# Weights' loads issued from ScalarE, new estimates for a planner, and short chunks of keys filled up, in an attention and MLP kernel

## The chip, the cores and the metric

One core of one Trainium2 chip. The metric is device time in microseconds of one execution, median over runs: 1034.23 us for the kernel before (1033.37 to 1034.86, three runs).

## The reference, cut to what matters

Inputs: local queries, keys and values (8 batches, 8 heads, 512 positions, 64 features), global ones (32 positions), and two weight matrices, 512 x 2048 and 2048 x 512, which arrive as 64-bit floats.

```python
k_all = concat([k_g, k_l]); v_all = concat([v_g, v_l])
out_g = softmax(scale * q_g @ k_all.T) @ v_all              # global queries see all keys
s_ll  = where(|i - j| <= 32, scale * q_l @ k_l.T, -1e9)     # local ones a band
s_l   = concat([scale * q_l @ k_g.T, s_ll])                 # and the 32 global keys
out_l = softmax(s_l) @ v_all
x = concat([out_g, out_l]) as (8 * 544 tokens, 8 heads * 64)
h = x @ w_in                                               # 512 -> 2048
g = h * tanh(softplus(h))                                  # mish
return g @ w_out                                           # 2048 -> 512
```

## The kernel before

**Tiling.** Heads are taken in pairs (`hp`, 4 for each batch `b`), called a head below. A unit is 128 local queries `t` of one head, 128 units in all. `scores` (lines 599 and 606) multiplies queries with a window of 192 or 224 key columns; `row_max` (VectorE), `expo` (ScalarE), `p_hi` and `p_lo` make two 16-bit parts `ph` of the probabilities; `p_turn` transposes them into `pt` by DMA; `pv` (line 657) multiplies `pt` with two chunks of values: `va` (rows by `CHK`: 96, 128, 128, 128 for the four tiles) and `vc` (96, 96, 96, 64), each with three products for high and low parts, in two halves of the head pair. That makes 12 small matmuls of 64 moving columns for a unit. `v_move` fills `va` and `vc` by DMA from `vf` and `vgf`. The global queries run once for each head: `g_scores`, `g_max`, `g_exp`, `g_norm`, `g_turn`, and `g_pv` (line 744), whose first chunk has 32 rows (partitions 96 to 127 of `va` and of `gpt`) and whose other four have 128.

**MLP.** Tokens go in 17 blocks of 256. For each block 8 steps: `m1_mm` (line 787), `mish` on ScalarE (line 830), `g_hi` and `g_lo`, `m2_mm` (line 855).

**Weights.** 32 halves of 512 KB each, 0 to 15 of the first matrix and 16 to 31 of the second. `w_load` brings one in by `load`, a DMA issued on the sync engine's queue (SP, line 294); `w_bits` and `w_sum` make 32-bit floats of it on VectorE, ScalarE and GpSimd; `w_stat` and `w_norm` work out a scale, with a reduction over partitions on GpSimd (line 414); `w_split` writes two 16-bit parts. Their raw bits lie in buffers that other tiles use later (`PLACE`). Batches' values have a scale too, by `b_max` and `b_scale` (reduction at line 490), used by `b_split` (line 510).

**Order.** `Plan` simulates the engines when the program is built: each task has an engine, a duration in ns, what it reads and writes, and a priority (its number, or, with `pl.slot`, a place counted in units of 37 tasks). `order` (line 133) takes the task that can start soonest, at equal time the one of lowest priority; the instructions of each engine are then put out in that order and each engine runs them in order, waiting where it must. DMAs are a fifth engine there, "DMA", issued on SP: one occupies it for `max(ns, DMA_MIN)` and is done `DMA_IN + ns + DMA_OUT` after its start (lines 191 to 193). A task on VectorE beside GpSimd is lengthened (line 190). The constants at lines 1013 to 1027 say where the weights' steps and the loads of later batches are placed.

Of the kernel before, what the change touches and what calls it, by code (L numbers as in the profile page):

```python
# [12 lines left out]
F16 = mybir.dt.float16  # L13
# [30 lines left out]
CHK = [(96, 96), (128, 96), (128, 96), (128, 64)]  # L44
# [6 lines left out]
class Plan:  # L51
# [5 lines left out]
    DMA_IN, DMA_OUT, DMA_MIN = 1650, 900, 650  # L57
# [75 lines left out]
    def order(self):  # L133
# [10 lines left out]
        columns = {}  # L144

# [17 lines left out]
        def first(e):  # L163

            best = None
            for pri, n, ns, t in queue[e]:
                t = max(t, free[e]) + (self.TABLE if e == ACT and self.tasks[n][7] not in (None, self.table) else 0)
# [12 lines left out]
        for _ in range(N):  # L180
            t, pri, e, n, ns = min(c for c in map(first, free) if c)
            start[n], on[n] = t, e
            if e == ACT:
                self.table = self.tasks[n][7] or self.table
# [4 lines left out]
            if e == DVE and free[POOL] > t:  # L189
                ns += 0.5 * min(ns, free[POOL] - t)  # L190
            if e == DMA:
                free[e] = t + max(ns, self.DMA_MIN)
                done[n] = t + self.DMA_IN + ns + self.DMA_OUT
            else:
                free[e] = done[n] = t + ns
# [19 lines left out]
def attn_mish_kernel(ctx: ExitStack, tc: tile.TileContext, qt, kt, qt0, kt0, vm, vg, qg, w1, w2, consts_in, out, w64):  # L215
    nc = tc.nc
# [19 lines left out]
    def rings(pool, *table):  # L236
        for tag, bufs, shape, dt in table:
# [11 lines left out]
          ("vf", 2, [128, 4, 2, 128], F16), ("va", 2, [128, 4, 2, 128], F16), ("vc", 2, [96, 4, 2, 128], F16),  # L249
# [14 lines left out]

    def kept(tag, bufs, shape):
# [5 lines left out]
    kept("ph", 2, [128, 2, 2, 256])  # L271
    kept("gph", 1, [64, 2, 640])
# [85 lines left out]
    def w_load(k):  # L358
        j, hf = HV[k]

        def go():
            n = 2 if w64 else 1
            dst = raw(k) if w64 else wf(k).bitcast(I32)
            if j < 8:
                load(dst.rearrange("p (c f) -> p c f", c=2),
                     w1[hf * 256:(hf + 1) * 256, j * 256 * n:(j + 1) * 256 * n].rearrange("(c p) f -> p c f", p=128))
            else:
                r0 = (j - 8) * 256 + hf * 128
                load(dst, w2[r0:r0 + 128, :])
        if w64:  # L370
            p = PLACE[k]
            pl.add(DMA, dma(512), go, w=[rawkey(k)] if p in range(18) else (), new=() if p in range(18) else [(p, ("wraw", k))])
        else:
            pl.add(DMA, dma(256), go, w=[wkey(j, hf)])
# [3 lines left out]
    def w_bits(k):  # L378
# [3 lines left out]
        pl.add(DVE, 335, lambda: V.tensor_scalar(f(), words(k)[:, :, 1], 3, 0x3FFFFFFF, ALU.logical_shift_left, ALU.bitwise_and),  # L382
# [4 lines left out]
    def w_sum(k):  # L387
# [3 lines left out]
        pl.add(DVE, 602, lambda: V.scalar_tensor_tensor(f(), words(k)[:, :, 1], -0x40000000, f(), ALU.bitwise_and, ALU.bitwise_or),  # L391
               r=[rawkey(k)], w=[key])
        pl.add(POOL, pool(512), lambda: G.tensor_tensor(f(), f(), X["wr", k], ALU.add), r=[("wr", k)], w=[key])  # L393
# [13 lines left out]
    def w_norm(w):  # L407
# [6 lines left out]
        pl.add(POOL, 600, lambda: G.partition_all_reduce(X[p], X[m], 128, RED.add), r=[m], new=[("p2", p)])  # L414
# [15 lines left out]
    def w_split(j):  # L430
# [9 lines left out]
        else:  # L440
            pl.add([(ACT, act(1024)), (DVE, dve2(1024))], 0, lambda e: scaled(e, f, f, c), r=[["sw", w]], w=[k])
            pl.add([(ACT, act(1024)), (DVE, dve2(1024))], 0, lambda e: copy(e, wh(j, 0), f), r=[k], w=[wslot(j)])
            pl.add(POOL, pool(1024) * 0.9, lambda: G.tensor_tensor(wh(j, 1), f, wh(j, 0), ALU.subtract), r=[k, hi], w=[lo])
# [701 lines left out]
```

## Time and profile before

| | us |
|---|---|
| median of three runs | 1034.23 |
| the profiled execution | 1032.9 |
| its span, first to last instruction | 1031.1 |
| TensorE busy (matmul) | 944.5, 92% |
| ScalarE busy | 681.1, 66% |
| VectorE busy | 665.0, 64% |
| GpSimd busy | 81.8, 8% |
| mean granted TensorE clock | 0.994 |

Line 855 and line 787 (the MLP) hold about 1050 us of matmul records that overlap one another, line 657 123 us, line 744 26 us. The shares are averages: the first fifth of the span looks different from the rest, so the profile is read by stretches of 20 us. All DMAs of the program run on one queue. In the rows PE is TensorE's matmul, PEld its weight load, DVE VectorE, ACT ScalarE, POOL GpSimd, SPq the issue of DMAs on the sync engine. In brackets stands the idle time of the engine ahead of a group and what ended it.

### The profile page before, as it was taken

How to read it: one execution, taken by the hardware profiler on the slowest of the kernel's cores; microseconds unless marked ns; L12 is line 12 of the kernel's file. 1: busy time of each engine (PE TensorE's matmuls, PEld its weight loads, DVE VectorE, ACT ScalarE, POOL GpSimd, SP SyncE). 2: the span in 40 equal slices, each digit the busy share in tenths (PEclk: the TensorE clock that was granted, in tenths of full speed). 3: DMA queues.
4: the chain of work that ended last, by engine and by line, in shares of the span. 5: the costliest groups of instructions: out<-in, count | busy, mean ns of one | idle time of the engine just before them, and what ended most of it. 6: DMA issues, size and time to landing. Idle time of an engine off the chain costs nothing.

```text
span 1031.1 us, 20578 instructions
## 1 busy us (share of the span) xinstructions
PE 944.5 (92%) x7906; PEld 670.3 (65%) x7906; DVE 665.0 (64%) x1704; ACT 681.1 (66%) x1321; POOL 81.8 (8%) x60
## 2 busy tenths in 40 slices
PE   3456797899999999999999999999999999999996
PEld 2234475566776777777767777777777777666663
DVE  6877896887667766776676666767676655422221
ACT  3465566666887788778878788787878788311110
POOL 2725222410000000000000000000000000000000
PEclk9999998999999999999999999999999999999998
DMA  9847983696758764766566665665576444100000
GB/s 333 220 115 171 281 233 78 121 187 155 165 105 176 144 143 105 182 141 141 116 163 148 131 131 129 159 128 133 119 162 125 116 75 79 38 11 21 1 21 21
DMA packets 231802, 134.65 MB, mean 131 GB/s; under 512 B 197528, under 2 KB 209048, under 8 KB 230680
## 3 DMA queue, kind: packets, MB, share of 16 engines
q1 hardware_dynamic: 231704, 133.34, 56.6%
q8 instruction: 62, 1.02, 0.4%
q14 instruction: 36, 0.29, 0.1%
HBM read 63.55 MB, written 8.91 MB: 70 GB/s over the span
## 4 chain that ended last, share of the span: by engine, by line
PE 71%; DVE 11%; DMA 7%; issue 2%; ACT 2%; SPq 1%; POOL 0%; ACTq 0%; DVEq 0%
PE o L855 29%; PE h L787 29%; PE U L657 4%; PE s L606 4%; DMA vraw<-in_vm 3%; PE g L695 2%; PE gu L744 2%; DMA gpt<-gph 2%; DVE vmx L479 1%; DMA pt<-ph 1%; DVE ph L640 1%; DVE P L612 1%; DVE ks L300 1%; DVE kl L544 1%; DMA wraw<-in_w 1%
## 5 line engine op out<-in xcount | busy, mean ns | idle before, releaser
L855 PE MATMUL o<-W,G 128*128 128x512 f16 x1632 | 389.9, 379 | 0.0
L787 PE MATMUL h<-xh,W 128*128 128x256 f16 x2048 | 379.3, 275 | 5.2 <-ACT e L830 5.1
L787 PEld LDWEIGHTS <-W 128*128 128x128 f16 x3264 | 310.9, 98 | 69.8 <-issue 5.5
L787 PE MATMUL h<-xl,W 128*128 128x256 f16 x1024 | 281.0, 274 | 0.0
L855 PEld LDWEIGHTS <-G 128*128 128x128 f16 x1632 | 156.8, 98 | 144.3 <-issue 0.3
L830 ACT ACTIVATE e<-h,c 128x512 f32<-128x512 f32 (+1 forms) x137 | 92.6, 683 | 117.0 <-PE h L787 115.9
L621 ACT ACTIVATE P<-P,nm 128x192 f32<-128x192 f32 (+1 forms) x256 | 117.8, 460 | 40.3 <-DVE nm L612 39.0
L612 DVE CUSTOM_DVE_ANT_0 P<-s,consts 128x192 f32<-128x192 f32 (+1 forms) x256 | 90.1, 367 | 79.3 <-PE s L606 70.2
L307 DVE TENSOR_SCALAR G<-e,c 128x512 f16<-128x512 f32 x129 | 63.2, 490 | 115.3 <-ACT e L830 115.1
L640 DVE SCALAR_TENSOR_TENSOR ph<-P,ph 128x384 f16<-128x384 f32 (+1 forms) x128 | 79.1, 619 | 82.0 <-ACT ph L305 81.3
L843 DVE SCALAR_TENSOR_TENSOR G<-e,c,G 128x512 f16<-128x512 f32 (+1 forms) x137 | 102.0, 744 | 3.4
L830 ACT ACT_TABLE_LOAD x79 | 101.4, 1283 | 1.4
L621 ACT ACT_TABLE_LOAD x74 | 94.9, 1283 | 1.4
L657 PEld LDWEIGHTS <-pt 96*128 96x128 f16 (+2 forms) x1536 | 64.1, 101 | 34.2 <-DMA pt<-ph 21.6
L305 ACT ACTIVATE ph<-P 128x384 f16<-128x384 f32 (+1 forms) x128 | 69.7, 547 | 16.3 <-DMA pt<-ph 13.2
L657 PE MATMUL U<-va,pt 128*128 128x64 f16 (+1 forms) x768 | 62.0, 200 | 14.8 <-DMA pt<-ph 12.5
L606 PE MATMUL s<-ks,qs 128*128 128x192 f32 (+1 forms) x216 | 71.4, 353 | 1.4 <-DVE qs L536 0.8
L657 PE MATMUL U<-vc,pt 96*128 96x64 f16 (+1 forms) x768 | 61.3, 198 | 0.0
L393 POOL TENSOR_TENSOR W<-W,wr 128x512 int32<-128x512 int32 x32 | 50.2, 1579 | 77.3 <-DVE W L391 42.4
L716 ACT ACTIVATE gP<-g,gmx 64x288 f32<-64x288 f32 x64 | 30.4, 476 | 37.8 <-DVE gmx L711 37.6
L606 PE MATMUL s<-kl,qs 128*128 128x192 f32 (+1 forms) x216 | 54.2, 274 | 0.0
L403 PE MATMUL ws<-W 128*128 128x128 bf16 x128 | 17.7, 285 | 37.0 <-POOL W L393 37.0
(102 smaller groups left out, 1016.6 us busy)
## 6 DMA issues: line engine op xcount, KB each, us to landing
kraw<-in_kt SPq DMA_DIRECT2D x27, 640.0 KB, 4.7
qraw<-in_qt SPq DMA_DIRECT2D x27, 512.0 KB, 4.1
W<-in_w SPq DMA_DIRECT2D x19, 512.0 KB, 6.1
out<-ob SPq DMA_DIRECT2D x34, 256.0 KB, 2.6
vraw<-in_vm SPq DMA_DIRECT2D x8, 1024.0 KB, 6.1
wraw<-in_w SPq DMA_DIRECT2D x13, 512.0 KB, 6.2
vc<-vf SPq DMA_DIRECT2D x32, 128.0 KB, 2.3
va<-vf SPq DMA_DIRECT2D x32, 96.0 KB, 2.3
```

Source lines behind the costliest of these rows:

```text
L305: A.activation(out=dst, in_=src, func=AF.Copy, scale=c)
L307: V.tensor_scalar(dst, src, c, None, ALU.mult)
L393: pl.add(POOL, pool(512), lambda: G.tensor_tensor(f(), f(), X["wr", k], ALU.add), r=[("wr", k)], w=[key])
L606: T.matmul(X[s][:, :w], X[qs][:, h, t * 128:(t + 1) * 128], X[k][:, h, c0:c0 + w], start=(i == 0), stop=(i == 1))
L612: pl.add(DVE, 69 + 1.04 * w, lambda: V.tensor_tensor_reduce(out=X[P][:, h, :w], in0=X[s][:, :w], in1=mask[:, m0:m0 + w], scale=-SCALE, sca ...
L621: pl.add(ACT, 160 + 0.832 * w + 93, lambda: A.activation(out=X[P][:, h, :w], in_=X[P][:, h, :w], func=AF.Exp, bias=X[nm], scale=-1.0, accu ...
L640: pl.add(DVE, dve(n), lambda: V.scalar_tensor_tensor(p_part(X[ph], t, 1), p_src(X[P], t), PSC, p_part(X[ph], t, 0), ALU.mult, ALU.subtract ...
L657: T.matmul(X[u][:, t, h, :], X[pt][:k, p * 4 + h * 2 + c, :], X[vx][:k, t, vl, h * 64:(h + 1) * 64], start=(n == 0), stop=(n == 5))
L787: T.matmul(X[h][:, f * TB:(f + 1) * TB], wh(i, wl)[:, off:off + 128], X[x][:, d, o:o + TB], start=(n == 0), stop=(n == 11))
L830: chain(blk, i, ACT, 571, lambda a, z: A.activation(out=X[e][:, a:z], in_=hv(blk, i)[:, a:z], func=AF.Mish, bias=0.0, scale=X[c][:, 0:1]), ...
L843: chain(blk, i, DVE, 602, lambda a, z: V.scalar_tensor_tensor(gp(1, blk, i)[:, a:z], X[e][:, a:z], X["c", blk][:, 2:3], gp(0, blk, i)[:, a ...
L855: T.matmul(X[o], gp(g, blk, i)[:, f, t * 128:(t + 1) * 128], wh(8 + i, wl)[:, f * 512:(f + 1) * 512], start=(i == 0 and n == 0), stop=(i = ...
```

## The change

Four parts. `w_load` issues its DMA from ScalarE, and the planner holds it for a task of ScalarE of the kind "dma", with an account of its own for the bytes moved. The planner's durations are set anew: DMA constants, transposes 8 ns for each KB instead of 5, the two reductions over partitions 4500 ns instead of 600, several steps of the weights, the lengthening beside GpSimd; and the constants that place the weights' steps and later batches' loads. The last tile's second chunk in `CHK` has 96 rows instead of 64, and `g_pv` multiplies all 128 rows of its first chunk instead of 32. For that, `vc` is a kept tile that is cleared once at the start, so rows that no move fills are zero; the first 96 columns of `gph` were cleared already.

```diff
-CHK = [(96, 96), (128, 96), (128, 96), (128, 64)]
+CHK = [(96, 96), (128, 96), (128, 96), (128, 96)]
-    DMA_IN, DMA_OUT, DMA_MIN = 1650, 900, 650
+    DMA_IN, DMA_OUT, DMA_MIN, DMA_AHEAD = 1300, 600, 620, 4000
...
+            if self.tasks[n][7] == "dma":
+                moved2 = max(moved2, t) + ns * 1.2
+                free[e] = t + self.DMA_MIN
+                done[n] = moved2 + self.DMA_IN + self.DMA_OUT
...
             if e == DVE and free[POOL] > t:
-                ns += 0.5 * min(ns, free[POOL] - t)
+                ns += 0.6 * min(ns, free[POOL] - t)
             if e == DMA:
-                free[e] = t + max(ns, self.DMA_MIN)
-                done[n] = t + self.DMA_IN + ns + self.DMA_OUT
+                moved = max(moved, t) + ns
+                free[e] = max(t + self.DMA_MIN, moved - self.DMA_AHEAD)
+                done[n] = moved + self.DMA_IN + self.DMA_OUT
...
-          ("vf", 2, [128, 4, 2, 128], F16), ("va", 2, [128, 4, 2, 128], F16), ("vc", 2, [96, 4, 2, 128], F16),
+          ("vf", 2, [128, 4, 2, 128], F16), ("va", 2, [128, 4, 2, 128], F16),
...
     kept("ph", 2, [128, 2, 2, 256])
+    kept("vc", 2, [96, 4, 2, 128])
     kept("gph", 1, [64, 2, 640])
...
             if j < 8:
-                load(dst.rearrange("p (c f) -> p c f", c=2),
+                nc.scalar.dma_start(dst.rearrange("p (c f) -> p c f", c=2),
...
             else:
                 r0 = (j - 8) * 256 + hf * 128
-                load(dst, w2[r0:r0 + 128, :])
+                nc.scalar.dma_start(dst, w2[r0:r0 + 128, :])
...
-            pl.add(DMA, dma(512), go, w=[rawkey(k)] if p in range(18) else (), new=() if p in range(18) else [(p, ("wraw", k))])
+            pl.add(ACT, dma(512), go, w=[rawkey(k)] if p in range(18) else (), new=() if p in range(18) else [(p, ("wraw", k))], table="dma")
...
-        pl.add(POOL, 600, lambda: G.partition_all_reduce(X[p], X[m], 128, RED.add), r=[m], new=[("p2", p)])
+        pl.add(POOL, 4500, lambda: G.partition_all_reduce(X[p], X[m], 128, RED.add), r=[m], new=[("p2", p)])
...
-        pl.add(DMA, kib * 5, lambda: nc.sync.dma_start_transpose(dst(), src()), r=r, w=w, new=new)
+        pl.add(DMA, kib * 8, lambda: nc.sync.dma_start_transpose(dst(), src()), r=r, w=w, new=new)
...
-        pl.add(POOL, 600, lambda: G.partition_all_reduce(X[p], X[m][:, 5:6], 128, RED.max), r=[m], new=[("p2", p)])
+        pl.add(POOL, 4500, lambda: G.partition_all_reduce(X[p], X[m][:, 5:6], 128, RED.max), r=[m], new=[("p2", p)])
...
             for c in range(5):
-                r = slice(0, 128) if c else slice(96, 128)
-                vv = X[vf][:, c - 1] if c else X[va][r, 1]
+                vv = X[vf][:, c - 1] if c else X[va][:, 1]
                 for p, vl in ((0, 0), (0, 1), (1, 0)):
-                    T.matmul(X[u][:, :64], vv[:, vl, :], X[pt][r, p * 5 + c, :], start=(n == 0), stop=(n == 14))
+                    T.matmul(X[u][:, :64], vv[:, vl, :], X[pt][:, p * 5 + c, :], start=(n == 0), stop=(n == 14))
...
-    RATE1 = 0.1
-    CONV2 = 8.279
+    RATE1 = 0.133
+    CONV2 = 7.324
...
-    FIRST1 = 10.551
-    STEP1 = 0.114
-    FIRST2 = 14.027
+    FIRST1 = 9.986
+    STEP1 = 0.14
+    FIRST2 = 13.099
     STEP2 = 0.833
-    AHEAD_DMA = 3.119
-    LATE_K = 11.02
-    LATE_L = 158.572
-    LATE_B = 8.569
-    LATE_V = 0.0
+    LOAD1 = -1.233
+    LOADS1 = 0.116
+    AHEAD_DMA = 7.181
+    LATE_K = 122.989
+    LATE_L = 168.71
+    LATE_B = 0.0
+    LATE_V = 294.429
...
         if a == "w":
+            pl.slot = LOAD1 + LOADS1 * n
             w_load(n)
+            pl.slot = None
```

## Rows read from the trace of the kernel before

**Rows 1.** Stretches of 20 us: PE, PEld, DVE, ACT, POOL busy; PEclk; DMA share; GB/s.

```profile
0.00:20.00 20.00, 9.32 (x26) 5.29 (x26) 11.99 (x40) 8.51 (x22) 3.78 (x8) 1.00 0.89 318
20.00:40.00 20.00, 8.75 (x46) 4.93 (x46) 15.95 (x31) 8.60 (x20) 14.08 (x10) 1.00 1.11 328
40.00:60.00 20.00, 6.47 (x40) 3.70 (x38) 13.62 (x29) 6.49 (x18) 8.47 (x7) 1.00 0.28 68
...
120.00:140.00 20.00, 16.59 (x113) 11.58 (x113) 19.19 (x40) 10.79 (x25) 7.68 (x6) 1.00 1.09 291
...
160.00:180.00 20.00, 14.87 (x125) 10.87 (x123) 12.09 (x32) 14.84 (x21) 3.91 (x4) 0.83 0.36 75
...
200.00:220.00 20.00, 17.99 (x144) 11.09 (x143) 14.82 (x43) 15.24 (x35) 4.29 (x2) 1.00 0.90 187
...
500.00:520.00 20.00, 20.00 (x183) 14.56 (x181) 14.27 (x37) 16.61 (x32) 0.00 (x0) 1.00 0.49 105
...
sum 1040.00, PE 944.52 PEld 670.27 DVE 665.01 ACT 681.07 POOL 81.79; mean PE 18.16 PEld 12.89 DVE 12.79 ACT 13.10 POOL 1.57
```

**Rows 2.** Timeline of TensorE, 506 to 515 us: start, duration, line, operation.

```profile
506.78 0.26 PE L657 MATMUL U<-va,pt 128*128 128x64 f16 x3
...
507.14 0.27 PE L787 MATMUL h<-xh,W 128*128 128x256 f16 x1
...
508.45 1.46 PE L855 MATMUL o<-W,G 128*128 128x512 f16 x6
509.75 0.27 PE L787 MATMUL h<-xh,W 128*128 128x256 f16 x1
...
511.06 1.46 PE L855 MATMUL o<-W,G 128*128 128x512 f16 x6
512.45 0.26 PE L744 MATMUL gu<-gpt,va 32*128 32x64 f16 x3
...
513.00 0.35 PE L606 MATMUL s<-ks,qs 128*128 128x224 f32 x1
...
513.52 0.26 PE L657 MATMUL U<-va,pt 128*128 128x64 f16 x3
...
514.29 0.28 PE L787 MATMUL h<-xh,W 128*128 128x256 f16 x1
```

**Rows 3.** Groups by line and shape, whole span: busy us, mean ns | idle.

```profile
L657 PE MATMUL U<-vc,pt 64*128 64x64 f16 x192 | 17.1, 198 | 0.0
...
L744 PE MATMUL gu<-gpt,va 32*128 32x64 f16 x96 | 8.5, 196 | 1.7 <-DMA gpt<-gph 1.7
```

**Rows 4.** Line 744 alone in stretches of 20 us: PE, PEld, PEclk, DMA.

```profile
200.00:220.00 20.00, 0.71 (x15) 0.54 (x15) 1.00 0.90 187
```

**Rows 5.** Timeline of GpSimd at the start.

```profile
0.72 1.84 POOL L268 MEMSET ph<- 128x1024 f16 x2 [0.29 <-POOLq L1134]
```

**Rows 6.** Timeline of all engines around 58 us, at the weights' first reduction.

```profile
58.23 0.15 DVE L415 TENSOR_SCALAR wp<-wp 128x1 f32<-128x1 f32 x1 [4.32 <-POOL wp L414]
...
58.74 1.01 PE L599 MATMUL s<-ks,qs 64*128 64x192 f32 x2 [4.25 <-DVE nm L612]
```

**Rows 7.** Timelines of ScalarE and of TensorE around 165 us.

```profile
164.40 0.40 ACT L510 ACTIVATE vgf<-vgraw,sv 128x128 f16<-128x128 f32 x1 [7.72 <-DVE sv L315]
...
166.65 0.37 PE L787 MATMUL h<-xh,W 128*128 128x256 f16 x1 [5.09 <-ACT e L830]
```

**Rows 8.** Chain that ended last, in order of time, 110 to 240 us.

```profile
166.65 8.18 PE h L787 x48
```

**Rows 9.** Instructions of wraw (min/median/max ns), then timeline of SP's issues and VectorE.

```profile
L294 SPq DMA_DIRECT2D wraw<-in_w x13: 328/577/1452, 4.2 to 137.2; - x13
...
18.16 5.11 SPq L294 DMA_DIRECT2D W<-in_w  x5
30.48 7.84 SPq L465 DMA_TRANSPOSE pt<-ph  x2
...
8.54 0.56 DVE L640 SCALAR_TENSOR_TENSOR ph<-P,ph 128x384 f16<-128x384 f32 x1
```

More of the change, by code (lines that the diff above doesn't have):

```diff
@@ L144, in order @@
         columns = {}
+        moved = moved2 = 0
         def tensor(t, ns, rows):
@@ L166, in first @@
             for pri, n, ns, t in queue[e]:
-                t = max(t, free[e]) + (self.TABLE if e == ACT and self.tasks[n][7] not in (None, self.table) else 0)
+                t = max(t, free[e]) + (self.TABLE if e == ACT and self.tasks[n][7] not in (None, "dma", self.table) else 0)
                 e0 = self.tasks[n][0][0][0]
@@ L182, in order @@
             start[n], on[n] = t, e
+            if self.tasks[n][7] == "dma":
+                moved2 = max(moved2, t) + ns * 1.2
+                free[e] = t + self.DMA_MIN
+                done[n] = moved2 + self.DMA_IN + self.DMA_OUT
+                queue[e] = [c for c in queue[e] if c[1] != n]
+                for u in users[n]:
+                    left[u] -= 1
+                    if not left[u]:
+                        enter(u)
+                continue
             if e == ACT:
@@ L368, in go @@
                 r0 = (j - 8) * 256 + hf * 128
-                load(dst, w2[r0:r0 + 128, :])
+                nc.scalar.dma_start(dst, w2[r0:r0 + 128, :])
         if w64:
             p = PLACE[k]
-            pl.add(DMA, dma(512), go, w=[rawkey(k)] if p in range(18) else (), new=() if p in range(18) else [(p, ("wraw", k))])
+            pl.add(ACT, dma(512), go, w=[rawkey(k)] if p in range(18) else (), new=() if p in range(18) else [(p, ("wraw", k))], table="dma")
         else:
-            pl.add(DMA, dma(256), go, w=[wkey(j, hf)])
+            pl.add(ACT, dma(256), go, w=[wkey(j, hf)], table="dma")
     def w_bits(k):
@@ L381, in w_bits @@
         f, key = lambda: wf(k).bitcast(I32), wkey(*HV[k])
-        pl.add(DVE, 335, lambda: V.tensor_scalar(f(), words(k)[:, :, 1], 3, 0x3FFFFFFF, ALU.logical_shift_left, ALU.bitwise_and),
+        pl.add(DVE, 360, lambda: V.tensor_scalar(f(), words(k)[:, :, 1], 3, 0x3FFFFFFF, ALU.logical_shift_left, ALU.bitwise_and),
                r=[rawkey(k)], w=[key])
@@ L390, in w_sum @@
         f, key = lambda: wf(k).bitcast(I32), wkey(*HV[k])
-        pl.add(DVE, 602, lambda: V.scalar_tensor_tensor(f(), words(k)[:, :, 1], -0x40000000, f(), ALU.bitwise_and, ALU.bitwise_or),
+        pl.add(DVE, 680, lambda: V.scalar_tensor_tensor(f(), words(k)[:, :, 1], -0x40000000, f(), ALU.bitwise_and, ALU.bitwise_or),
                r=[rawkey(k)], w=[key])
-        pl.add(POOL, pool(512), lambda: G.tensor_tensor(f(), f(), X["wr", k], ALU.add), r=[("wr", k)], w=[key])
+        pl.add(POOL, 1400, lambda: G.tensor_tensor(f(), f(), X["wr", k], ALU.add), r=[("wr", k)], w=[key])
     def w_stat(k):
@@ L442, in w_split @@
             pl.add([(ACT, act(1024)), (DVE, dve2(1024))], 0, lambda e: copy(e, wh(j, 0), f), r=[k], w=[wslot(j)])
-            pl.add(POOL, pool(1024) * 0.9, lambda: G.tensor_tensor(wh(j, 1), f, wh(j, 0), ALU.subtract), r=[k, hi], w=[lo])
+            pl.add(POOL, 2230, lambda: G.tensor_tensor(wh(j, 1), f, wh(j, 0), ALU.subtract), r=[k, hi], w=[lo])
     LO, HI = slice(0, 64), slice(64, 128)
```

## The prediction

> **What bounds the kernel now.** I read the stretches of 20 us first, for which engine is full where. From 220 us to the end TensorE is busy for the whole of nearly every stretch: 20.00 of 20.00 in 500 to 520, at a granted clock of 1.00, 2.4 GHz [rows 1]. VectorE (14.27) and ScalarE (16.61) have room there. Before that TensorE is half idle: 9.32, 8.75 and 6.47 us of the first three stretches, 14.87 of 160 to 180 [rows 1]. Over the span it is busy 944.52 us of 1031.1, so it idles 86.6 us, and the eleven stretches up to 220 us, of which the first and the last stand in the rows, hold 72.4 of these. The end can therefore come sooner in two ways only: TensorE gets less work after 220 us, or it waits less before. I look at the first with the timeline of TensorE in the steady part, at the second with the waits and the timeline of the start.
>
> **Filling the short chunks.** The timeline of TensorE shows two prices for the same twelve instructions. Line 657 makes four groups of three small products for each tile of 128 queries. Tiles whose chunks have 128 and 96 rows: first start at 506.78, next work at 507.14, so 0.36 us, 0.030 each. The last tile of a head, with chunks of 128 and 64 rows: 513.52 to 514.29, 0.77 us [rows 2]. Going from 128 to 96 rows costs nothing; going to 64 rows and back costs about 0.1 us each time, and the last tile does so four times. Filling the 64 to 96 makes it a tile like the others: 0.77 - 0.36 = 0.41 us less for each head.
>
> Line 744 starts with three products of 32 rows. It takes from 512.45 to 513.00, 0.55 us for 15 products; at 0.030 each it would be 0.45, so 0.10 of that is the way back to 128 rows. The way there lies ahead of it: six products of line 855 that are followed by a 128-row product take 508.45 to 509.75, 1.30 us, those that are followed by the 32-row ones 511.06 to 512.45, 1.39 us, 0.09 more [rows 2]. Together 0.19 us for each head, and 0.60 with the tile above. There are 192 matmuls with 64 rows and 96 with 32 rows, six and three for each of 32 heads [rows 3]; their count stays, only their rows grow, and I cost the added rows at nothing, since 96- and 128-row products already run at the same 0.030.
>
> Heads in the full part: six stretches up to 220 us hold 15 matmuls of line 744 each, the last of them that of [rows 4], so 6 of the 32 groups lie before and 26 after. 26 x 0.60 = **15.6 us less**, one for one, since no other engine is near full there. What covers this: ScalarE at 16.61 of 20 goes to about 17. For the other 6 heads (3.6 us) TensorE waits anyhow; I take 0 and keep 0 to 3.6. Padding also needs zeroed rows in vc: two more clears on GpSimd. The two clears of ph, of the same length per partition, take 1.84 us at the very start [rows 5], where nothing has landed that GpSimd could work on; hidden. Without that cover it would be 1.8 us once.
>
> The Trainium skill (TensorEngine Tiling (Array Packing), Key Properties) says that a change of tiling mode drains the engine, which the 0.1 us agrees with. The same page (Theoretical Speedup) speaks against filling: 64 and 32 rows may run up to 2 and 4 times faster. By it the change would forfeit 192 x 0.015 + 96 x 0.022 = 5 us, an estimate from that page; no group in the trace shows such a speed-up.
>
> **The planner's estimates.** The planner builds the order of every engine from its own durations, so a wrong one puts an instruction that must wait in front of others on an in-order engine. It gave the reduction over partitions 600 ns. In the trace VectorE idles 4.32 us until the weights' first one is done, and TensorE 4.25 us at the same place [rows 6]. The second is worse: ScalarE waits 7.72 us at line 510 for a scale from the next reduction, and behind it in its queue is the mish whose result TensorE needs; TensorE idles 5.09 us, and the next 48 products of line 787 run partly at the lower level of the clock, 1.2 GHz (0.83 on average in 160 to 180) [rows 1, 7]. They take 8.18 us [rows 8], where the steady rate is 1.31 for 12 (511.06 less 509.75 [rows 2]), 5.2 for 48, so 2.9 lost. Sum of what the right estimate (4500 ns) could remove: 4.25 + 5.09 + 2.9 = 12.2 us. The other way the bound is a plan that helps nowhere, 0. I take half, **6 us less**: when these waits are filled VectorE is next, with 15.95 of 20 in 20 to 40 and 19.19 in 120 to 140 [rows 1], and work moved into a gap still has to be work that TensorE was waiting for. The other estimates (transposes, splits, vector operations beside GpSimd) and the new places of the weights' steps only change this same order; they have no rows of their own, and their spread goes into the range.
>
> **The weights' loads on ScalarE.** 32 instructions leave SP's queue and enter ScalarE's. On SP one takes 0.33 to 1.45 us, 0.58 at the median [rows 9]: 32 x 0.58 = 18.5 us of ScalarE's time, 10.5 to 46 at the ends. The first sixteen are the dear ones: five took 5.11 us [rows 9], because the DMA engines were full: 318 and 328 GB/s in the first two stretches [rows 1]. ScalarE is busy 8.51, 8.60 and 6.49 us of the first three stretches [rows 1], so there is room, but each load stands in order: what is queued behind it on ScalarE is the exponentials of the first tiles and the low words of the weights, for which the probabilities' transposes and GpSimd's sums wait. Loads 16 to 31 also wait until a buffer is read out; on SP transposes were behind them, now the exponentials and the mish are. In return SP is free: in the trace the first two transposes of probabilities are issued at 30.48 and take 7.84 us, although a first low part of ph is written at 8.54 [rows 9]; loads and moves stood before them. Bounds: a gain up to the TensorE idle time of 20 to 60 us, 24.8 us [rows 1]; a loss up to 16 x 1.45 = 23 us. I take **0**: nearest are the rows of these stretches, in which the DMA engines, not an issuing queue, were full until 40 us.
>
> Sum against the profiled execution, 1032.9 us (span 1031.1 and 1.8 around it): 1032.9 - 15.6 - 6 = 1011.3. The median of the runs is 1.3 us above that execution, so **1012.6**, I say 1012.
>
> **Rivals.**
> *The plan books two queues, the chip has one set of engines.* The new planner keeps a separate account for ScalarE's loads, as if they moved beside SP's. In the first two stretches 318 and 328 GB/s [rows 1] were the sum of all. Sixteen loads of 0.52 MB are 8.4 MB, 26 us at 323 GB/s; keys, queries and values of batch 0, about 3.8 MB by their shapes in the code, are 12 us more. Booked side by side they end at 26, on the chip at 38, so work placed by the plan may wait up to 12 us on ScalarE and VectorE. Then the 6 us are gone and up to 12 added: 1034.2 - 15.6 + (0 to 12) = 1019 to 1031, middle 1025. For it: every early step hangs on loads. Against it: in the kernel before the loads took as long, and VectorE was behind them anyway. The Trainium skill states the rule (DMA: Bandwidth & Descriptors, Issuing engines are not separate DMA queues): issuing from another engine saves only the issue time; the trace of before has all its loads on one queue and can't show it.
>
> *The start gets much better.* SP's freedom lets the first tiles' results come tens of us sooner, and with them the first layer. All 12.2 us, the 3.6 and a third of the 24.8: 1034.2 - 15.6 - 12.2 - 3.6 - 8 = 995. Against it: VectorE's fill.
>
> *ScalarE blocks (slower than before).* At its place, the first 25 us, the loads hold ScalarE as long as they held SP at worst, 16 x 1.45 = 23 us, and no exponential gets in between; all of batch 0 shifts by that. With the 15.6 and without the 6: 1034.2 + 23 - 15.6 = 1042. It decides for slower once the shift is over 15.6 us. Against it: ScalarE is idle for more than half of these stretches, and the plan places first tiles' exponentials by their order among the loads.
>
> *The filling doesn't remove the price:* if the 0.1 us came from the weight loads of another tensor and not from the row count, the 15.6 would stay; then 1034.2 - 6 = 1028. Against it: 128 to 96 rows changes the tensor too and costs nothing [rows 2].
>
> **How the numbers follow.** Forecast, 1003 to 1018: 0.60. Two queues booked, 1018 to 1031: 0.21. Start much better, under 1003: 0.12. Filling worth nothing: 0.03, most of it near no change. Slower: 0.04. The range for 8 in 10: 1000 to 1026; it takes in the forecast, half of the much better start and most of the second case. A measurement of this kernel can tell about 0.2% from no change: faster 0.93, same 0.03, slower 0.04.
>
> **What would show it.** In the profile after: line 657's 64-row form and line 744's 32-row form are gone, and the last tile of a head goes by in 0.36 us; TensorE's full part is 15 us shorter. VectorE's and ScalarE's waits for a reduction of 4 to 8 us are gone or cover nothing of TensorE. Idle time of TensorE up to 220 us falls from 72 to about 66. Loads are listed on ScalarE's queue at 0.3 to 1.5 us each, with its first exponential near 7 us still; if that comes after 15 us, the blocking case holds. The prediction is wrong if TensorE's early idle time moves by over 12 us either way, or if ScalarE becomes full after 220 us.

## The result and the profile after

The changed kernel takes 1037.41 us (median; 1034.86 to 1039.48) where the kernel before takes 1034.23. The ratio is 1.0025, with a 95% interval of 1.0013 to 1.0037: a little slower. The forecast was 1012 us. The profiled execution has a span of 1037.7 us, 1039.48 as a run: it is the slowest of the thirteen, 2.1 us above the median, while the profiled one of the kernel before lies 1.3 below its median. So 3.4 us of what the two profiles differ by are spread between runs.

The price of a tile in the steady part went as forecast. The timeline of TensorE (start, us, engine, line, operation, out<-in, shape, count), the last tile of a head, line 657 before and 671 now:

```profile
511.13 0.26 PE L671 MATMUL U<-va,pt 128*128 128x64 f16 x3
511.23 0.25 PE L671 MATMUL U<-vc,pt 96*128 96x64 f16 x3
511.32 0.25 PE L671 MATMUL U<-va,pt 128*128 128x64 f16 x3
511.40 0.25 PE L671 MATMUL U<-vc,pt 96*128 96x64 f16 x3
511.50 0.27 PE L800 MATMUL h<-xh,W 128*128 128x256 f16 x1
```

0.37 us in place of 0.77 [rows 2]. The groups by line and shape hold the 64- and 32-row products of [rows 3] no more:

```profile
L671 PE MATMUL U<-vc,pt 96*128 96x64 f16 x768 | 58.9, 198 | 0.0
...
L757 PE MATMUL gu<-gpt,va 128*128 128x64 f16 x96 | 8.4, 199 | 2.2 <-DMA gpt<-gph 2.1
```

The start went otherwise. Stretches of 20 us, columns as in [rows 1]:

```profile
0.00:20.00 20.00, 4.76 (x16) 2.75 (x16) 10.07 (x24) 2.61 (x3) 6.63 (x11) 1.00 0.93 347
20.00:40.00 20.00, 3.26 (x14) 1.65 (x14) 4.25 (x12) 3.74 (x10) 2.60 (x3) 1.00 1.04 393
...
100.00:120.00 20.00, 10.00 (x94) 6.86 (x91) 19.94 (x32) 13.01 (x25) 10.20 (x5) 0.50 0.89 210
120.00:140.00 20.00, 10.84 (x73) 6.61 (x72) 19.83 (x47) 12.38 (x31) 9.07 (x6) 0.50 0.71 161
160.00:180.00 20.00, 15.59 (x119) 12.80 (x118) 13.42 (x40) 16.92 (x24) 3.23 (x3) 0.83 0.30 82
...
500.00:520.00 20.00, 20.00 (x175) 14.91 (x173) 14.53 (x42) 17.39 (x31) 0.00 (x0) 1.00 0.52 110
```

In the first 40 us TensorE is busy 8.0 us where it was 18.1, VectorE 14.3 where it was 27.9, ScalarE 6.4 where it was 17.1. Then VectorE is full from 100 to 140 us, and TensorE's clock is at its lower level there. Why the start is empty shows on three engines. ScalarE, with its own issues (ACTq):

```profile
0.75 5.64 ACTq L379 DMA_DIRECT2D wraw<-in_w  x4
7.96 7.48 ACTq L379 DMA_DIRECT2D W<-in_w  x3
...
24.14 0.46 ACT L635 ACTIVATE P<-P,nm 128x192 f32<-128x192 f32 x1 [3.21 <-DVE W L396]
```

The first exponential starts at 24.14 us (6.90 before). GpSimd, where the bracket holds the idle time before a row and what ended it:

```profile
19.65 2.67 POOL L407 TENSOR_TENSOR W<-W,wr 128x512 int32<-128x512 int32 x2 [1.44 <-ACT wr L398]
31.51 0.38 POOL L504 PARTITION_ALL_REDUCE p<-vmx  x1 [9.19 <-issue]
40.84 3.77 POOL L407 TENSOR_TENSOR W<-W,wr 128x512 int32<-128x512 int32 x3 [8.96 <-issue]
...
166.30 0.40 POOL L428 PARTITION_ALL_REDUCE wp<-wm  x1 [6.48 <-issue]
```

Before, batch 0's reduction came at 13.32, ahead of all sums. Now it stands between two of them: 9.19 us go by before it and 8.96 after it in which GpSimd waits for nothing that the profile shows. VectorE stands still for both, the second time by way of ScalarE, where the scaling of the values is queued behind a conversion that waits for that sum; it has little else:

```profile
31.92 0.15 DVE L508 TENSOR_SCALAR p<-p 128x1 f32<-128x1 f32 x1 [6.57 <-POOL p L504]
...
43.13 0.35 DVE L526 SCALAR_TENSOR_TENSOR vgf<-vgraw,sv,vgf 128x128 f16<-128x128 f32 x1 [9.69 <-ACT vgf L524]
```

The weights' first reduction moves from 57.8 to 72.2 us, the first product of the first layer from 131.8 to 151.8. Of TensorE's waits that end between 40 and 240 us, those for GpSimd's sums are 47.8 us, 22.9 before (us in total, times, longest; before, then changed):

```profile
PE ws L403 <- POOL W L393: 22.9, 16, 3.3
```

```profile
PE ws L417 <- POOL W L407: 47.8, 17, 17.9
```

The longest, 17.9 us, ends at 42.15 and so lies mostly in the first 40 us; without it the sums cost 29.9.

The slow products behind 165 us [rows 8] are still there; 36 of them take 6.92 us, in the chain that ended last:

```profile
171.67 6.92 PE h L800 x36
```

Where TensorE idles tells the stages apart. The table is worked out from the stretches: their length less TensorE's busy time. The last column is its busy time. All kernels of the next part stand in it; their times are medians, and "less before" is against the kernel before in the same set of runs.

| kernel | us | less before | ratio, 95% | idle 0-40 | 40-100 | 100-180 | 180-240 | from 240 | busy |
|---|---|---|---|---|---|---|---|---|---|
| before | 1034.2 | | | 21.9 | 28.1 | 17.7 | 4.7 | 14.1 | 944.5 |
| **after** | 1037.4 | +3.2 | 1.0013-1.0037 | 32.0 | 24.6 | 27.6 | 4.9 | 22.0 | 926.6 |
| e1_fill | 1021.8 | -12.4 | 0.985-0.988 | 22.3 | 29.5 | 22.2 | 5.4 | 17.5 | 923.3 |
| e8_act | 1049.8 | +16.3 | 1.014-1.018 | 31.6 | 31.3 | 32.0 | 9.7 | 20.4 | 925.4 |
| e5_est | 1034.2 | +0.7 | 0.999-1.002 | 26.0 | 29.3 | 26.5 | 4.9 | 20.1 | 924.6 |
| est600 | 1031.1 | -3.0 | 0.996-0.998 | 23.8 | 28.4 | 29.1 | 2.2 | 21.7 | 924.0 |
| e6_places | 1041.0 | +7.5 | 1.006-1.009 | 21.7 | 29.3 | 43.3 | 1.4 | 18.7 | 925.7 |
| e7_late | 1031.9 | -1.7 | 0.998-1.000 | 22.3 | 28.9 | 31.3 | 2.2 | 16.3 | 929.2 |
| e2_sp | 1040.4 | +6.1 | 1.003-1.007 | 26.0 | 29.8 | 35.1 | 2.9 | 21.0 | 922.8 |
| e3_first_sp | 1036.1 | +1.8 | 1.000-1.003 | 25.1 | 27.4 | 34.5 | 1.5 | 19.6 | 923.0 |
| e4_red_first | 1043.4 | +9.1 | 1.005-1.010 | 29.2 | 27.0 | 41.6 | 0.0 | 21.6 | 922.2 |
| d_dve | 1033.0 | -1.1 | 0.997-0.999 | 22.7 | 31.9 | 24.7 | 6.9 | 18.5 | 926.8 |
| t_after | 1034.4 | +0.3 | 0.999-1.002 | 32.0 | 25.1 | 25.0 | 4.8 | 22.2 | 925.3 |
| c_hop | 1024.5 | -8.9 | 0.989-0.993 | 22.6 | 27.8 | 22.4 | 4.5 | 18.4 | 926.6 |
| c_next | 1020.5 | -12.9 | 0.986-0.990 | 22.2 | 29.7 | 20.7 | 2.7 | 17.1 | 925.2 |
| s_switch | 1019.2 | -14.2 | 0.984-0.988 | 22.1 | 27.5 | 17.9 | 2.7 | 17.5 | 929.6 |
| p_wb | 1028.7 | -4.7 | 0.994-0.997 | 21.8 | 27.8 | 29.0 | 3.4 | 18.3 | 928.0 |
| s_after | 1040.6 | +6.6 | 1.005-1.008 | 30.2 | 22.3 | 19.1 | 12.4 | 30.7 | 923.9 |
| a_ahead | 1050.5 | +15.4 | 1.010-1.019 | 31.3 | 24.6 | 42.8 | 7.1 | 24.1 | 923.4 |
| a_one | 1054.1 | +19.1 | 1.016-1.021 | 31.2 | 36.6 | 33.0 | 4.9 | 21.6 | 922.3 |

From before to after TensorE has 18.0 us less to do, and idles 10.1 us more in the first 40 us, 9.9 more from 100 to 180, 0.2 more from 180 to 240 and 7.9 more from 240 on, 3.5 less from 40 to 100: together 6.6 us more span. Of the waits from 240 us on, one kind is new, the first layer's products waiting for ScalarE's mish:

```profile
PE h L800 <- ACT e L843: 6.6, 5, 1.6
```

### The profile page after: what moved, and what is told of

It reads as the page before. It is cut to its first block, busy times and chain, and to the rows that moved or that the text cites. A ratio compares the mean times of both kernels' runs of the same rounds, so it can differ in the third digit from the quotient of the medians.

```text
span 1037.7 us, 20569 instructions
## 1 busy us (share of the span) xinstructions
PE 926.5 (89%) x7906; PEld 665.6 (64%) x7906; DVE 664.3 (64%) x1697; ACT 686.4 (66%) x1327; POOL 85.2 (8%) x62
## 3 DMA queue, kind: packets, MB, share of 16 engines
q10 hardware_dynamic: 6656, 16.78, 5.0%
## 4 chain that ended last, share of the span: by engine, by line
PE 61%; DVE 11%; DMA 8%; ACT 6%; SPq 2%; issue 2%; POOL 0%; ACTq 0%; DVEq 0%; POOLq 0%
PE o L868 26%; PE h L800 25%; PE s L620 4%; DMA vraw<-in_vm 3%; PE U L671 3%; PE g L709 2%; DMA gpt<-gph 2%; SPq L308 2%; ACT L843 1%; PE gu L757 1%; DVE ph L654 1%; DVE P L626 1%; DVE vmx L493 1%; DMA W<-in_w 1%; ACT e L843 1%
## 5 line engine op out<-in xcount | busy, mean ns | idle before, releaser
L635 ACT ACTIVATE P<-P,nm 128x192 f32<-128x192 f32 (+1 forms) x256 | 118.0, 461 | 34.8 <-DVE nm L626 29.9
L671 PEld LDWEIGHTS <-pt 96*128 96x128 f16 (+1 forms) x1536 | 59.3, 101 | 28.0 <-DMA pt<-ph 20.4
L671 PE MATMUL U<-va,pt 128*128 128x64 f16 (+1 forms) x768 | 59.5, 200 | 16.4 <-DMA pt<-ph 15.1
L671 PE MATMUL U<-vc,pt 96*128 96x64 f16 x768 | 58.9, 198 | 0.0
L407 POOL TENSOR_TENSOR W<-W,wr 128x512 int32<-128x512 int32 x32 | 48.3, 1520 | 80.6 <-DVE W L405 17.7
L417 PEld LDWEIGHTS <-W 128*128 128x128 bf16 x128 | 10.9, 127 | 67.5 <-POOL W L407 65.1
(102 smaller groups left out, 1049.8 us busy)
```

The costliest lines, as they stand in the source:

```text
L407: pl.add(POOL, 1400, lambda: G.tensor_tensor(f(), f(), X["wr", k], ALU.add), r=[("wr", k)], w=[key])
L635: pl.add(ACT, 160 + 0.832 * w + 93, lambda: A.activation(out=X[P][:, h, :w], in_=X[P][:, h, :w], func=AF.Exp, bias=X[nm], scale=-1.0, accu ...
L671: T.matmul(X[u][:, t, h, :], X[pt][:k, p * 4 + h * 2 + c, :], X[vx][:k, t, vl, h * 64:(h + 1) * 64], start=(n == 0), stop=(n == 5))
```

## The experiments

Two theories stood first. *The loads:* ScalarE is held by them, and taking them back to the sync engine gives the time back. *The plan:* the new estimates and places spoil the order, whoever loads.

**The filling alone** (e1_fill): before with the filled chunks, old estimates and places, loads on the sync engine.

```diff
-CHK = [(96, 96), (128, 96), (128, 96), (128, 64)]
+CHK = [(96, 96), (128, 96), (128, 96), (128, 96)]
```

> The kernel before with the filling alone: 96 rows in the last tile's second chunk, 128 rows in the first chunk of the global queries, vc cleared once; loads on SP, old estimates, old places. If the filling is worth what the rows of before say (0.60 us for each of 26 heads in TensorE's full part), the time is 1034.2 - 15.6 = 1018.6, between 1015 and 1020. If the filling gives its gain back as idle time of TensorE in the full part, as the changed kernel seems to show (926.5 us busy, but 8 us more idle after 240 us), 1026.

1021.8 us, 12.4 less than before. Stretches after 240 us, before and then filled, columns as above:

```profile
240.00:1040.00 800.00, 776.96 (x6638) 557.20 (x6636) 474.58 (x1255) 539.03 (x1007) 1.76 (x5) 1.00 0.51 111
```

```profile
240.00:1040.00 800.00, 762.81 (x6643) 552.99 (x6640) 475.02 (x1255) 539.25 (x1009) 1.75 (x5) 1.00 0.51 111
```

TensorE has 14.2 us less to do and idles 3.4 more. The waits of TensorE from 240 us on (us in total, times, longest) name it: the transposes, 2.6 and 0.8 us before.

```profile
PE U L658 <- DMA pt<-ph: 4.1, 6, 1.5
PE gu L744 <- DMA gpt<-gph: 2.7, 5, 1.2
```

The time lies between the two cases of the expectation, and the three other parts of the change take 15.6 us.

**All loads back, or the first sixteen** (e2_sp, e3_first_sp), and **the sums held behind batch 0's reduction** (e4_red_first), each an edit of the changed kernel.

```diff
-                nc.scalar.dma_start(dst.rearrange(...), ...)
+                nc.sync.dma_start(dst.rearrange(...), ...)      # e3: if k < 16
-  pl.add(POOL, 1400, ..., r=[("wr", k)], w=[key])
+  pl.add(POOL, 1400, ..., r=[("wr", k)] + ([("sv", 0)] if k < 16 else []), w=[key])   # e4
```

> The changed kernel with all 32 loads of the weights back on SP and booked there (the first 16 without a place of their own, in the order of the list); new estimates, new places and filling stay. Theory 1, ScalarE's queue holds up the start (first exponential at 24.1 us against 6.9, VectorE 13.6 us less work done in the first 40 us): VectorE's work of the first 40 us is back at about 28 us, the first product of line 800 comes near 132 to 138 us instead of 151.8, and the time is 1037.4 - 20 = 1017, between 1012 and 1022. Theory 2, the new places and estimates are what puts VectorE's work into a worse order: still over 1028.

> As the run before, but only the first 16 loads are back on SP; those of the second matrix stay on ScalarE. Theory 1 says that the first 30 us do the harm: the same time as with all on SP, within 4 us. If the loads of the second matrix are at fault (ScalarE waits in order for a buffer, VectorE idle 140 to 150 us while a load takes 9.2 us to land), 1030 or more.

> The changed kernel, loads still on ScalarE, with one more dependence: GpSimd's sums of the first matrix wait in the plan for batch 0's scale, so GpSimd makes the reduction over partitions ahead of all sums, as in the kernel before. In the changed kernel three sums come first, the reduction stands 9.2 us idle ahead of it and the next sum 9.0 us behind it. Theory 3, the early loss is GpSimd's changes between sums and reduction: 9 us of GpSimd's time come back, and with them about 9 us of the end, 1028. Theory 1: ScalarE is held by its loads all the same, the time stays within 4 us of 1037.

1040.4, 1036.1 and 1043.4 us. With all loads on the sync engine the first exponential is at 6.0 us and batch 0's reduction at 13.9, and yet the kernel is no faster: 6 us less idle before 40, 7.5 more from 100 to 180. The loads as the one cause fall: that theory asked for 1012 to 1022. The third theory, GpSimd's changes, asked for 1028 once the reduction goes ahead of the sums; it does so in e4_red_first (15.40 us), and the kernel is 6 us slower. e3_first_sp is 4.3 us below e2_sp, just outside the 4 us that its expectation allowed.

**Each remaining part alone, on the filling:** the estimates (e5_est), all but the reduction's (est600), the places (e6_places), the four late ones among them (e7_late), the loads on ScalarE (e8_act).

```diff
+    e5:  DMA_IN, DMA_OUT, DMA_MIN, DMA_AHEAD = 1300, 600, 620, 4000; reductions 4500; transposes kib * 8; ...
+    est600: as e5, with the reductions at 600
+    e6:  RATE1 ... LATE_V as in the change
+    e7:  LATE_K, LATE_L, LATE_B, LATE_V = 122.989, 168.71, 0.0, 294.429
+    e8:  nc.scalar.dma_start in w_load, with the plan's account for it
```

> Filling and the new estimates of the planner (durations, DMA account, 0.6 beside GpSimd), but loads on SP and the weights' and later batches' steps at their old places. The filling alone gave 1021.8, filling with estimates, places and loads on SP 1040.4. If the new places cause the 18.6 us between them: 1018 to 1024 here. If the estimates alone do: 1036 to 1042. If it takes both, something between.

> Filled chunks with all new estimates but that of the reduction (600 ns as before), loads on the sync engine, old places; with the reduction at 4500 it was 1034.2 us. If the reduction's new estimate is what costs the 12 us: 1020 to 1025. If the other estimates (transposes 8 a KB, splits, loads booked ahead) cost them: 1030 to 1038.

> Filling and the new places (RATE1 to LATE_V), with the old estimates and loads on SP. If the new places cause the 18.6 us: 1036 to 1042. If the estimates do: 1018 to 1025.

> Filling and of the new places only the four for later batches (LATE_K 123, LATE_L 168.7, LATE_B 0, LATE_V 294); the weights' steps at their old places, old estimates, loads on SP. If the later preparation of batch 1 starves TensorE after 130 us, most of the loss of the new places is here too, over 1030, and the second batch's first products come later than 175 us; if the earlier weights' steps are at fault, 1019 to 1025.

> Filling and all 32 loads on ScalarE, booked there as in the changed kernel, with the old estimates for everything else, the old places and the first 16 loads in the order of the list. If the moving of the loads does harm by itself, as the first 30 us of the changed kernel look (first exponential at 24 us): 1030 to 1040. If, as the two runs with loads back on SP say, it hardly matters for the end: 1018 to 1026.

Against the filling alone, each with its own set of runs: estimates +13.1 us, all but the reduction's +9.4, places +19.9, the late ones +10.7, loads +28.7; all parts together +15.6. They do not add up: each is harmful alone, and why they cost so much less together isn't shown. The places of the first sixteen loads (`LOAD1`, `LOADS1`) are in none of these five kernels; they have a say further down.

The four with estimates or places keep the start (idle before 40 us 21.7 to 26.0, 22.3 with the filling alone) and lose 4.3 to 21.1 us from 100 to 180. In that stretch e5_est has no wait of TensorE over 3.7 us; the others have a long one, another one every time (est600, e6_places, e7_late; of the second kind the filling alone has 5.1 us):

```profile
PE U L672 <- DMA va<-vgf: 8.1, 1, 8.1
```

```profile
PE h L787 <- ACT e L830: 13.4, 1, 13.4
```

```profile
PE o L855 <- POOL W L444: 9.0, 1, 9.0
```

For the places the trace shows what lies behind the wait. With the filling alone GpSimd makes the weights' second reduction and batch 1's side by side, so it changes once for both; in e6_places they are 20 us apart, with subtractions (line 444) between them. GpSimd, filled and then e6_places:

```profile
163.90 0.40 POOL L415 PARTITION_ALL_REDUCE wp<-wm  x1 [6.93 <-issue]
164.22 0.44 POOL L491 PARTITION_ALL_REDUCE p<-vmx  x1
```

```profile
140.65 0.40 POOL L415 PARTITION_ALL_REDUCE wp<-wm  x1 [7.91 <-issue]
...
160.63 0.38 POOL L491 PARTITION_ALL_REDUCE p<-vmx  x1 [6.49 <-issue]
167.75 2.50 POOL L444 TENSOR_TENSOR W<-W 128x1024 f16<-128x1024 f32 x1 [6.75 <-issue]
```

ScalarE waits 5.35 us for that last row, with the mish that TensorE needs (175.92) behind it in its queue: an in-order queue stands behind an instruction that is placed too early. In e7_late the two reductions are 7.7 us apart (151.25 and 158.91), and TensorE's 9.0 us end with the first subtraction after them. What makes the waits of the estimates isn't shown; their reductions stay side by side.

The loads alone lose at the start instead. ScalarE of e8_act:

```profile
0.75 5.65 ACTq L377 DMA_DIRECT2D wraw<-in_w  x4
8.12 16.33 ACTq L377 DMA_DIRECT2D W<-in_w  x9
...
29.38 0.44 ACT L633 ACTIVATE P<-P,nm 128x192 f32<-128x192 f32 x1
```

Nine loads in a row hold ScalarE for 16 us, 1.81 us each. Behind them wait the first exponential (29.38) and the weights' first conversion (28.26), so also GpSimd's first sum (29.01) and the reduction after it, for which VectorE idles 19.8 us; VectorE is busy 10.2 us of the first 40 (25.1 with the filling alone).

**Is VectorE's time at the start worth what the loss suggests?** On the filling, same written order, VectorE's step of the first sixteen loads is done twice (d_dve); in the changed kernel it is left out for the last sixteen (t_after).

```diff
-        pl.add(DVE, 602, lambda: V.scalar_tensor_tensor(f(), ...), ...)
+        pl.add(DVE, 602, lambda: [V.scalar_tensor_tensor(f(), ...) for _ in range(2 if k < 16 else 1)], ...)
-        pl.add(DVE, 680, lambda: V.scalar_tensor_tensor(f(), ...), ...)
+        pl.add(DVE, 680, lambda: k < 16 and V.scalar_tensor_tensor(f(), ...), ...)   # t_after
```

> Filled chunks alone (1021.8 us), the same written order; the 0.69 us step of VectorE that sums a weight's words is done twice for the first sixteen loads, 11 us more of VectorE before 50 us and nothing else. If time that VectorE loses at the start isn't made up (VectorE is the bound of the whole head): 1029 to 1033. If VectorE has slack there and another engine or a load sets the pace: 1021 to 1025.

> The changed kernel (1037.4 us), the same written order; it leaves out VectorE's sum of the words of loads 16 to 31 (a part of the weights' conversion), 16 x 0.69 = 11 us less of VectorE between 70 and 150 us. If VectorE sets the pace of its head (it is full from 100 to 140 us): 1026 to 1031. If loads or GpSimd set it: 1034 to 1038.

11 us more at the start cost 11 us (1033.0); 11 us less from 70 to 150 us give 3 (1034.4). The first is one to one though VectorE looks idle for a third of 20 to 60 us in the filled kernel. The timelines of VectorE and of GpSimd say why; the filled kernel:

```profile
36.37 0.68 DVE L392 SCALAR_TENSOR_TENSOR W<-W 128x512 int32<-128x512 int32 x1
...
39.42 1.63 DVE L392 SCALAR_TENSOR_TENSOR W<-W 128x512 int32<-128x512 int32 x1
40.98 0.42 DVE L383 TENSOR_SCALAR W<-W 128x512 int32<-128x512 int32 x1
```

```profile
39.20 1.31 POOL L394 TENSOR_TENSOR W<-W,wr 128x512 int32<-128x512 int32 x1 [0.69 <-DVE W L392]
41.20 1.31 POOL L394 TENSOR_TENSOR W<-W,wr 128x512 int32<-128x512 int32 x1 [0.69 <-DVE W L392]
```

and with the doubled step, GpSimd:

```profile
44.30 1.31 POOL L394 TENSOR_TENSOR W<-W,wr 128x512 int32<-128x512 int32 x1 [1.42 <-DVE W L392]
47.03 1.31 POOL L394 TENSOR_TENSOR W<-W,wr 128x512 int32<-128x512 int32 x1 [1.42 <-DVE W L392]
```

VectorE's step takes 0.68 us by itself and 1.63 beside GpSimd's sum. The two make one chain of 2.00 us for each load, 2.73 with the doubled step, and everything after it shifts by 10 us (the first layer's first product from 133.0 to 143.3). In the changed kernel this chain is what GpSimd's detour to the reduction and back interrupts: no sum starts between 22.3 and 40.84 us. From 70 us on VectorE does not set the pace there, or for little of the time: of 11 us taken from it 3 come back, although it is full from 100 to 140.

**Do GpSimd's changes, or any new order, cost the time?** On the filling: two planner constants moved by 2% (c_hop, c_next), GpSimd's changes priced in the plan as a state of the engine (s_switch), the early reductions on TensorE (p_wb); on the changed kernel the same price (s_after).

```diff
-    HOP = 170
+    HOP = 173                               # c_hop
-    NEXT = {..., DVE: 127, ...}
+    NEXT = {..., DVE: 130, ...}             # c_next
+                if e == POOL and (self.tasks[n][7] == "red") != self.lib:
+                    t += 7500 if self.lib else 6300            # s_switch, s_after
-        pl.add(POOL, 600, lambda: G.partition_all_reduce(X[p], X[m], 128, RED.add), ...)
+        pl.add(PE, 60, lambda: T.matmul(X["ws", w][:, 128:129], ones, X[m], start=True, stop=True), ...)   # p_wb
```

> Control: the kernel with the filled chunks alone (median 1021.8 us), with one constant of the planner moved by 2%: the price of a hop between engines 173 ns instead of 170. No work is added or removed, only the written order differs. Theory A (the plan is fitted to its own order, any new order is worse by some 10 us): 1027 to 1040. Theory B (the losses of the changed kernel come from GpSimd's changes between sums and reductions and from what waits on the weights): 1020 to 1025, with the first weight step of TensorE (m1) near 133 us.

> A second control: filled chunks alone, with VectorE's price between two instructions 130 ns instead of 127 in the planner. Theory A (fitted plan): 1027 to 1040, by another amount than the first control. Theory B (GpSimd's changes and the weights): 1020 to 1025.

> Filled chunks alone, with GpSimd's change from sums to a reduction priced in the planner at 6300 ns and the way back at 7500 ns, as the traces show them, as a state of the engine (the reduction itself stays at 600). Theory A: a new order all the same, 1027 to 1040. Theory B: the planner puts the reductions next to each other or where nobody waits, 1012 to 1020.

> Filled chunks alone, with the four early reductions across partitions (both weights', and those of batches 0 and 1, there a sum in place of a maximum, which is an upper bound and changes that batch's scale alone) made by TensorE with a matrix of ones, so that GpSimd changes to no reduction while the weights are summed. Theory B: the 6 to 9 us going in and 7 to 11 us coming out are saved at each, part of it on the path: 1005 to 1016. Theory A: 1027 to 1040, a new order. If neither the order nor the changes matter: 1020 to 1023.

> The changed kernel with its reductions at 600 ns and GpSimd's changes priced in the planner, 6300 ns into a reduction and 7500 ns out of it. If these changes, of which the new estimate has only the way in, are what spoils its order: 1022 to 1030, with the first reduction ahead of the sums again. If not: 1034 to 1042.

1024.5, 1020.5, 1019.2, 1028.7 and 1040.6 us. A small disturbance of the constants costs 0 to 4 us, and s_switch, a new order too, costs nothing, so "any other order loses 10 us" falls as a rule. p_wb alone lies in that theory's range, 7.8 us above the filling alone, and far from the 1005 to 1016 that theory B asked of it. Without reductions GpSimd's gaps are gone, as its timeline shows (before: a reduction at 57.79 and the next sum at 66.69):

```profile
50.50 1.51 POOL L396 TENSOR_TENSOR W<-W,wr 128x512 int32<-128x512 int32 x1 [0.69 <-DVE W L394]
60.93 1.65 POOL L396 TENSOR_TENSOR W<-W,wr 128x512 int32<-128x512 int32 x1 [8.91 <-ACT wr L387]
```

but the sum then waits for ScalarE, and from 90 to 185 us TensorE waits 19.3 us for the sums (9.7 with the filling alone):

```profile
PE ws L406 <- POOL W L396: 19.3, 9, 7.7
```

So the gaps are real, and removing them in this way, which also changes the order and adds products to TensorE, wins nothing. Priced in, it gives the best time (1019.2, ratio 0.9857), which can't be told from the filling alone or c_next. In the changed kernel the reduction does go ahead of the sums (15.18 us) and idle from 100 to 180 us falls to 19.1; the time is lost elsewhere, 12.4 us from 180 to 240 and 30.7 after.

**Which fault of the plan empties the start of the changed kernel?** ScalarE held as long as its booked loads ask (a_ahead), or one account for the loads of both engines (a_one).

```diff
-                free[e] = t + self.DMA_MIN
+                free[e] = max(t + self.DMA_MIN, moved2 - self.DMA_AHEAD)     # a_ahead
-                moved2 = max(moved2, t) + ns * 1.2
+                moved = max(moved, t) + ns                                    # a_one, and done[n] from moved
```

> The changed kernel, where the planner holds ScalarE after a load until the loads that it booked there are within 4000 ns of their end, about 1.7 us for each load in a row (the trace has 1.8 us from issue to issue), in place of 620 ns. If the unpriced hold on ScalarE spoils the start: first exponential before 15 us, VectorE busy over 20 us of the first 40, 1022 to 1031. If not: 1034 to 1042.

> The changed kernel, where the planner books ScalarE's loads and the sync engine's into one account, as one set of DMA engines moves them; ScalarE is still held for 620 ns only. If booking two queues side by side is the fault: 1022 to 1031. If the hold on ScalarE is: 1034 to 1042, with a first exponential near 24 us still.

1050.5 and 1054.1 us: worse, and outside both ranges of the expectations. The first exponential of a_ahead stays at 24.36 us, VectorE at 15.6 us of the first 40; in a_one they are at 18.83 and 19.9, and TensorE's idle time before 40 us stays at 31.2 (32.0 in the changed kernel). The first exponentials, a_ahead and a_one:

```profile
24.36 0.46 ACT L635 ACTIVATE P<-P,nm 128x192 f32<-128x192 f32 x1 [2.36 <-DVE W L396]
```

```profile
18.83 0.44 ACT L635 ACTIVATE P<-P,nm 128x192 f32<-128x192 f32 x1
```

With the hold priced in, the plan still doesn't put the exponentials ahead. The written order says why. In the changed kernel and in the five edits of it that keep these loads on ScalarE at their new places (e4_red_first, t_after, s_after, a_ahead, a_one), exactly twelve loads stand ahead of the first exponential on ScalarE. Load n (from 0) has the place `LOAD1 + LOADS1 * n`, in units of 37 tasks: the twelfth is at 1.6 tasks, the thirteenth at 5.9, and the first exponential is the fifth task of the first tile, at 4. When ScalarE is free in the plan and both could start, the lower number goes first, whatever either is booked at. In e8_act, where the sixteen loads have their place in the list, ahead of all tiles, all sixteen stand ahead. So it is the loads' places that keep the exponentials back, and neither of the two faults tested; what later places would give no run shows.

## Why the prediction was wrong, step by step

**Filling: right, size a little off.** 15.6 us were forecast; TensorE's work after 240 us fell by 14.2, 0.57 us for each of the 25 heads there in place of 0.60. The last tile is as forecast (0.37 us). "One for one, since no other engine is near full there" was the weak half: 3.4 us came back as waits, most of them for transposes. Net 12.4. The rival "filling doesn't remove the price" is out. The faster small tiles of the Trainium skill (TensorEngine Tiling (Array Packing), Theoretical Speedup) don't show: the 64-row products took 198 ns each [rows 3], the 96-row ones take 198.

**Estimates: the sign failed.** The step took half of a bound of 12.2 and set the other end at 0, "a plan that helps nowhere". Nothing excluded a loss: a new plan can place an instruction badly anywhere. Alone, the estimates cost 13.1 us. The step also looked at the wrong one: the reduction's estimate, to which the whole 6 us were tied, adds 3.7 to the 9.4 that the others cost without it, and those had "no rows of their own" and went into the range. The new places had no term; alone they cost 19.9. What failed is not that the named waits go: from 40 to 240 us VectorE's for the weights' reductions fell from 8.7 (filling alone) to 2.0 in e5_est, TensorE's for the mish from 5.1 to 1.5. But the second fell in est600 too (1.1), where the reductions are still at 600, and TensorE's idle time came back elsewhere: in e5_est 3.7 us before 40, 4.3 from 100 to 180 and 2.6 from 240 on. In the changed kernel the 5.09 us at 165 us [rows 7] went down to 4.4 only. The 4500 ns are still short of the way in (6.48 and 9.19 us in the changed kernel), and nothing stands for the way out; with both priced (s_after) the changed kernel was no better, so that this is what spoils its order isn't shown.

**Loads on ScalarE: taken at 0, with bounds of 24.8 gained to 23 lost.** Alone they cost 28.7, beyond the bound, and the mechanism is that of the rival "ScalarE blocks": its sign, a first exponential after 15 us, came true (24.14). "ScalarE is idle for more than half of these stretches" [rows 1] was read as room. On an in-order engine the question is what stands behind the waiting instruction: the first sixteen loads left ScalarE over 27 us, though each issue took 0.4 us. The price per load was too low as well: 0.58 us at the median and 1.45 at worst, from thirteen issues on SP [rows 9], where nine in a row took 1.81 each on ScalarE. And the argument against the rival, that the plan places the exponentials "by their order among the loads", was true and worked for it: that order put them behind twelve. That rival had 23 us and 1042 in sum, and a chance of 0.04; the kernel measured 1037. The first 40 us cost TensorE 10.1 us in the changed kernel and 9.3 in e8_act, not 23; the rest of the 28.7 comes later. That 1042 is near the measured time is partly luck: its sum has neither the cost of the estimates nor that of the places, and with the loads back on the sync engine and these kept it is 1040.4.

**The sum.** It took the parts as independent. Alone they cost 13.1 + 19.9 + 28.7 = 61.7 us, together 15.6.

**Two queues booked.** That rival had the loss on ScalarE and VectorE up to 12 us, and VectorE did lose 13.6 in the first 40. But with one account the time rose to 1054; the cause it names isn't shown.

**What shows it.** The prediction called itself wrong if TensorE's early idle moved by over 12 us. It went from 72.4 to 89.1 (up to 240 us), with the clock at 1.2 GHz from 92 to 157 us. The clock is a small part at most: TensorE's busy time, which holds what slower products cost, is 3.2 us above that of the filled kernel in all, and that kernel was granted 0.61 on average from 100 to 140 us, the kernel before 1.00, while its first product of the first layer came 1.2 us later.

**Open.** Why the new estimates alone lose 9 to 13 us where small disturbances lose 0 to 4, and why estimates, places and loads together lose far less than their sum; the stalls are different instructions each time. And what the change would be worth with the loads placed behind the first exponentials.

## What to carry to other kernels

A repeated step in the part where one engine is full can be priced from two instances in the timeline, and holds within a tenth; expect part of it back as new waits, a quarter here. Idle time of an in-order engine is not room: before moving an instruction that can block, list what stands behind it and who waits for that, and look at which of two ready instructions the planner takes first. New constants of a planner are a new program: bound them on both sides by the stalls that such an order can make, don't add their parts, and measure each part alone before keeping them together; here the filling alone (1021.8 us) was worth more than the whole change.

## What the runs showed of the hardware

GpSimd's change between tensor operations and a reduction over partitions costs 6.0 to 9.2 us going in and 7.0 to 10.1 coming out, marked as waiting for nothing the profile shows (rows of before, after, e5_est and e8_act); the reduction itself takes about 0.4 in most rows. One row of e5_est, the first sum after batch 0's reduction:

```profile
23.83 3.76 POOL L408 TENSOR_TENSOR W<-W,wr 128x512 int32<-128x512 int32 x3 [10.09 <-issue]
```

VectorE's 128x512 int32 step takes 0.68 us alone and 1.63 beside GpSimd's sum of 1.31: the two hardly overlap.

Loads issued by ScalarE go through a queue of their own (16.78 MB), and the first 40 us moved 370 GB/s in place of 323 (347 in e8_act; 309 in a_ahead and 329 in a_one, so the queue alone doesn't give the rate). The Trainium skill (DMA: Bandwidth & Descriptors, Issuing engines are not separate DMA queues) says that such issuing saves only the time of the issue; that the same engines carry both agrees with the sixteenth load being out at 28 us, where it was out at 27 on the sync engine; the higher rate isn't what it leads one to expect.
